# Retention and a mixture of four experts on one core: expert outputs added up in DRAM by accumulating DMAs, and two more down projections in seven products

## The chip, the cores and the metric

The kernel runs on one core of a Trainium2 chip. The metric is the device time of one execution in microseconds. Before the change three runs gave 520.82, 521.08 and 521.61 us; the median is 521.08.

A core has several engines that run side by side and wait for one another through semaphores: PE (TensorE, matrix products into PSUM), PEld (TensorE's load of the stationary operand), DVE (VectorE, elementwise), ACT (ScalarE, elementwise, with a scale per partition), POOL (GpSimd, elementwise on SBUF only) and SP (SyncE, which here only issues DMAs). Each engine executes its own instructions in the order in which the program lists them. DMAs are issued from a queue of SP, ACT or POOL.

## The reference, cut to what matters

```python
# attention, for each of 8 batches and 8 heads: q, k, v are 576 x 64
scores = (q @ k.T) / sqrt(64)
ret = scores * gamma[h] ** (i - j) where i >= j, else 0
x = (ret @ v), heads side by side          # 4608 tokens x 512

# mixture of 4 experts on every token
p = domain_probs / (domain_probs.sum(-1) + 1e-9)
for e in range(4):
    h = maximum(x @ w1[e], 0)              # 512 -> 1024, "up"
    out += p[:, e:e+1] * (h @ w2[e])       # 1024 -> 512, "down"
```

Every token passes through all four experts, and the output of a token is a sum over the experts of a scaled down projection.

## The kernel before, in words

The 4608 tokens are cut into nine tiles `nt` = 0 to 8 of 512 tokens (`NT`), and each tile into four sub-tiles `ns` of 128 (`NSUB`). Tile and expert together make a stage (nt, e). Tile 0 and stage (1, 0) form the head, where the weights are loaded and the first attention is done. From (1, 1) on one loop runs over the stages, each in two halves g = 0 and 1. A half calls `up_fast`, the up projection of this stage, and in its four gaps (`fill(1)` to `fill(4)`) places a quarter each of the *down* projection of the stage before it.

An up projection computes one 2 x 2 block product in seven products of blocks in place of eight, by sums of blocks that are formed beforehand (`weight_sums`, `token_sums`). A down projection comes in two forms. The classical one, `downs`, takes 32 matmuls of 512 columns per tile and expert (line L541), four sub-tiles one after another. The other, class `Down`, takes seven products: 56 matmuls of 256 columns (L623), plus sums of the weights (`down_sums`, once an expert) and of the hidden layer (`hidden_sum`, L593 to L599, each stage), plus copies on ACT and two additions on DVE (L640). One `Down` covers sub-tiles s and s+2 and takes one half of a stage. The dictionary `begin` says from which tile on an expert's down projections take this form. `owed` lists the weight sums that are still to be formed, each with the earliest stage in which it may run (the last classical user of a block that is overwritten must be done) and the stage before which it must have run; `pay` takes the next one when DVE has a free slot, or all that are due when a stage starts.

The order of the work is written out by hand. Within a half, TensorE does product P, R, then fill 1 (products 1 and 5 of the down projection), P again, Q, fill 2 (6 and most of 2), P again, R, fill 3 (the rest of 2, and 7), P again, fill 4 (3 and 4). ACT copies Q from P (L678) and m5 from R (L680), applies the Relus (L686, L695, L700) and makes the copies of `Down` (L629, L633, L636); DVE forms R = P + m5 (L684), on which the following P product waits, and the fourth quarter of the hidden layer (L692), which POOL clips at zero (L693). In between the class `Chain` feeds attention for later tiles into all engines: casts of loaded q, k and v on POOL (L279, L281), transposes by DMA on SP (L297), scores, states and outputs on TensorE (L328 to L379), masks, running sums, and the writing of x for the tile (L242, ACT). When a tile's x is complete, four token sums (L569 to L572) follow on DVE; at the start of an expert-0 stage all that are left run at once.

A down projection ends with the evacuation from PSUM, in which the result is scaled by p. For expert 0 the scaled result is written into `acc`, one buffer of 128 x 512 for each sub-tile: `Down.out` does the first of its two sub-tiles on DVE (L652) and the second on ACT (L650); `downs` uses ACT (L529). For experts 1 to 3 DVE adds the scaled result to `acc` (L654 in `Down.out`, L531 in `downs`). After expert 3 the buffer is stored to `out` by a DMA from SP (L657, L534). Four buffers (`apool`, bufs = NSUB) serve one tile at a time. The helper `after(ins, dep)` makes one instruction wait for another.

Of the kernel before, what the change touches and what calls it, by code (L numbers as in the profile page):

```python
# [9 lines left out]
FP32 = mybir.dt.float32  # L10
# [4 lines left out]
MULT = mybir.AluOpType.mult  # L15
ADD = mybir.AluOpType.add
# [7 lines left out]
def kernel(  # L24
# [10 lines left out]
    nc = tc.nc  # L35
    B, H, S, D = q.shape
    N, E = moe_domain_probs.shape
    _, Dm, F = moe_w1.shape
# [8 lines left out]
    NFC = F // 128  # L47
    NT = 512
    n_nt = N // NT
    NSUB = NT // 128  # L50
# [8 lines left out]
    att1 = ctx.enter_context(tc.tile_pool(name="att1", bufs=1))  # L59
    att2 = ctx.enter_context(tc.tile_pool(name="att2", bufs=2))  # L60
    hpool = ctx.enter_context(tc.tile_pool(name="hpool", bufs=2))
    apool = ctx.enter_context(tc.tile_pool(name="apool", bufs=NSUB))
    xpool = ctx.enter_context(tc.tile_pool(name="xpool", bufs=3))
    tpool = ctx.enter_context(tc.tile_pool(name="tpool", bufs=1))
    psum = ctx.enter_context(tc.tile_pool(name="psum", bufs=1, space=PSUM))
# [6 lines left out]
    def bank(ring, shape, dtype, name):  # L72
        tag = RINGS[ring][turn[ring] % len(RINGS[ring])]
        turn[ring] += 1
        return psum.tile(shape, dtype, tag=tag, name=name)
# [4 lines left out]
    def after(ins, dep):  # L80
        tc.add_manual_dep(ins.ins, dep.ins.name,
                          mybir.DependencyInfo(mybir.DependencyClass.Sync, mybir.DependencyReason.DATA),
                          reason="start order")
# [58 lines left out]
    w1_sb, w2_sb = [], []  # L142
# [71 lines left out]
    probs = const.tile([128, E, NTT], FP32)  # L214
# [36 lines left out]
    class Att:  # L251


        def __init__(self, b):
            self.b, self.t = b, state[b]
            self.m, self.qkT, self.sT, self.s = {}, {}, {}, {}
# [235 lines left out]
                put_x(nc.vector, slice(2 * u, 2 * u + 2), self.b * S + 256 * hf + c * C, os[c])  # L492


    acc, hTs, tsum, ssum, dsum, hsum = {}, {}, {}, {}, {}, {}

    def up_classical(nt, e, lead=0, cut=NT // 2, pause=False):
# [21 lines left out]
    def downs(nt, e, ring):  # L519

        hT = hTs[nt, e]
        if e == 0:
            acc[nt] = [apool.tile([128, Dm], FP32, tag="acc", name="acc") for _ in range(NSUB)]

        def evacuate(po, ns, cols):
            t = nt * NSUB + ns
            pe, a = probs[:, e, t:t + 1], acc[nt][ns][:, cols]
            if e == 0:
                nc.scalar.activation(a, po, Copy, scale=pe)  # L529
            else:  # L530
                nc.vector.scalar_tensor_tensor(a, po, pe, a, op0=MULT, op1=ADD)  # L531
            if e == E - 1:
                eng = nc.scalar if cols.start else nc.sync
                eng.dma_start(out=out[t * 128:(t + 1) * 128, cols], in_=a)  # L534

        for ns in range(NSUB):
            w = Dm // 2 if (nt, ns, e) == (n_nt - 1, NSUB - 1, E - 1) else Dm
            for d in range(0, Dm, w):
                po = bank(ring, [128, w], FP32, "po")
                for fc in range(NFC):  # L540
                    nc.tensor.matmul(po, lhsT=hT[:, fc, ns * 128:(ns + 1) * 128],  # L541
                                     rhs=w2_sb[e][:, fc, d:d + w], start=(fc == 0), stop=(fc == NFC - 1))
                    yield None if fc < NFC - 1 else lambda: evacuate(po, ns, slice(d, d + w))

    def down_groups(nt, e):
        for f in downs(nt, e, "mm"):
            if f:
                f()
                yield
# [51 lines left out]
    class Down:  # L601
# [2 lines left out]

        def __init__(self, nt, e, s, tags=("o0", "o1")):
            self.nt, self.e, self.s, self.tags = nt, e, s, tags
            if e == 0 and s == 0:
                acc[nt] = [apool.tile([128, Dm], FP32, tag="acc", name="acc") for _ in range(NSUB)]

        def product(self, i, part=slice(0, NFC // 2)):  # L610
            hT, h, w, t = hTs[self.nt, self.e], hsum[self.nt, self.e], w2_sb[self.e], dsum[self.e]
# [28 lines left out]
            nc.vector.tensor_tensor(o, i, x, op=ADD)  # L640

        def out(self, i, halves=(slice(0, 2),)):
            ns = 2 * i + self.s
            t, po = self.nt * NSUB + ns, (self.V, self.W)[i]
            pe = probs[:, self.e, t:t + 1]
            for x in halves:
                cols = slice(x.start * HD, x.stop * HD)
                a, src = acc[self.nt][ns][:, cols], po[:, x].rearrange("p a d -> p (a d)")
                if self.e == 0 and i == 1:
                    nc.scalar.activation(a, src, Copy, scale=pe)  # L650
                elif self.e == 0:
                    nc.vector.tensor_scalar_mul(a, src, pe)  # L652
                else:
                    nc.vector.scalar_tensor_tensor(a, src, pe, a, op0=MULT, op1=ADD)  # L654
                if self.e == E - 1:
                    eng = nc.scalar if len(halves) == 1 and x.start else nc.sync
                    eng.dma_start(out=out[t * 128:(t + 1) * 128, cols], in_=a)  # L657

    def up_fast(nt, e, g, fill, window, sums):

# [315 lines left out]
    def stage(nt, e):  # L976
        return nt * E + e

    begin = {1: (1, 1), 2: (1, 2), 3: (2, 3), 0: (3, 0)}
    owed = [((1, 1), (2, 0), s0[3])]  # L980
    for e in (3, 0):

# [12 lines left out]
    for nt, e in [(nt, e) for nt in range(1, n_nt) for e in range(E)][1:]:  # L995
        fast = before >= begin[before[1]]
        fill_classical = None if fast else downs(*before, "po")
        while pay(nt, e, late=True):
            pass
# [142 lines left out]
```

## Time and profile before

| | before |
|---|---|
| median of three runs | 521.08 us |
| the profiled execution, in all | 521.82 us |
| its span | 520.1 us |
| TensorE busy | 505.5 us (97%) |
| VectorE busy | 388.8 us (75%) |
| ScalarE busy | 308.7 us (59%) |
| GpSimd busy | 196.1 us (38%) |
| stores of `out` from SP | 32 of 256 KB, median 2.9 us to landing; 8 of 128 KB, 1.8 us |
| DMA traffic | 54.24 MB, mean 104 GB/s |

The profile is of one execution. Its span begins with the first instruction and ends with the last; the execution's own time is 1.7 us longer. Busy time is the time in which an engine has an instruction under way. Matmuls overlap with one another, so that the duration of one (273 ns for 256 columns) is longer than the distance to the next; the pace is read from runs of several. A few matmul records are missing from the trace (214 of 224 in group L541). In a group's row the numbers after the bar are busy us, mean ns of one, and the idle time of the engine ahead of these instructions with what ended it.

### The profile page before, as it was taken

What the parts mean: (1) busy time and instruction counts of PE and PEld (TensorE: products, weight loads), DVE (VectorE), ACT (ScalarE), POOL (GpSimd) and SP (SyncE); (2) the same over time, 40 slices, a digit from 0 to 9 for tenths busy, and PEclk for the clock granted to TensorE, in tenths of its full rate; (3) what the DMA queues carried; (4) which work ended last, traced back from release to release, by engine and by line L of the source; (5) the groups of instructions that cost most, each with busy time, mean ns of one, the idle gap of its engine ahead of it and who ended that gap; (6) DMA issues with size and microseconds to landing.
All of it is one profiled execution on the core that took longest, in us unless ns stands there. A gap on an engine that the chain in (4) does not pass through costs nothing.

```text
span 520.1 us, 12551 instructions
## 1 busy us (share of the span) xinstructions
PE 505.5 (97%) x4871; PEld 401.6 (77%) x4886; DVE 388.8 (75%) x720; ACT 308.7 (59%) x637; POOL 196.1 (38%) x299
## 2 busy tenths in 40 slices
PE   8999999999999999999999999999999999999995
PEld 3644455678667878888888888888888888888884
DVE  6624579877646888779877987887788878787776
ACT  3462264666446756666666666766666667666661
POOL 6702275644433444444443543354345310000010
PEclk9999999999999999999999999999999999999999
DMA  9999998926183145525463538433941020011002
GB/s 239 187 208 201 199 204 184 160 48 113 42 203 62 42 101 134 137 57 114 95 159 72 112 70 196 72 89 65 204 95 42 13 80 2 2 41 42 2 1 82
DMA packets 149836, 54.24 MB, mean 104 GB/s; under 512 B 131308, under 2 KB 144620, under 8 KB 149776
## 3 DMA queue, kind: packets, MB, share of 16 engines
q1 hardware_dynamic: 142448, 45.05, 40.1%
q0 software_dynamic: 7328, 8.39, 9.5%
q8 instruction: 38, 0.62, 0.5%
q14 instruction: 22, 0.18, 0.1%
HBM read 45.16 MB, written 9.44 MB: 105 GB/s over the span
## 4 chain that ended last, share of the span: by engine, by line
PE 89%; DVE 7%; issue 2%; DMA 1%; ACT 0%; DVEq 0%; SPq 0%
PE upP L672 20%; PE downV L623 18%; PE downW L623 13%; PE upR L672 10%; PE po L541 8%; PE ph L500 6%; PE upQ L672 5%; PE s L328 2%; DVE acc L654 1%; PE oc L379 1%; PE kvp L346 1%; DVE upR L684 1%; PE oc L376 1%; DMA raw<-in_q_dram 1%; DVE sT L333 1%
## 5 line engine op out<-in xcount | busy, mean ns | idle before, releaser
L672 PEld LDWEIGHTS <-wt 128*128 128x128 bf16 x992 | 94.9, 98 | 18.0 <-issue 3.8
L623 PEld LDWEIGHTS <-hT 128*128 128x128 bf16 x928 | 90.8, 98 | 11.1 <-issue 0.6
L693 POOL TENSOR_SCALAR hT<-hT 128x512 bf16<-128x512 bf16 x62 | 38.3, 618 | 160.5 <-DVE hT L692 160.4
L672 PEld LDWEIGHTS <-wsum 128*128 128x128 bf16 x744 | 72.7, 98 | 12.2 <-issue 2.6
L623 PE MATMUL downV<-wt,hT 128*128 128x256 bf16 x464 | 78.4, 273 | 0.4 <-DVE acc L654 0.4
L672 PE MATMUL upP<-xT,wt 128*128 128x256 bf16 x496 | 74.4, 272 | 2.1 <-DVE upR L684 1.7
L623 PEld LDWEIGHTS <-hsum 128*128 128x128 bf16 x696 | 67.8, 98 | 8.7 <-DVE hsum L593 0.3
L684 DVE TENSOR_TENSOR upR<-upP,m 128x512 f32<-128x512 f32 x62 | 43.1, 696 | 35.8 <-PE upP L672 22.1
L700 ACT ACTIVATE hT<-upP 128x512 bf16<-128x512 f32 x62 | 37.0, 597 | 53.0 <-PE upP L672 39.2
L695 ACT ACTIVATE hT<-upR 128x512 bf16<-128x512 f32 x62 | 37.0, 597 | 32.7 <-PE upR L672 32.6
L541 PE MATMUL po<-wt,hT 128*128 128x512 bf16 x214 | 52.1, 379 | 0.6
L678 ACT ACTIVATE upQ<-upP 128x512 f32<-128x512 f32 x62 | 36.3, 586 | 26.0 <-PE upP L672 25.9
L340 POOL TENSOR_SCALAR_AFFINE_SELECT sT<-sT 128x512 bf16<-128x512 bf16 x24 | 15.2, 634 | 96.1 <-ACT sT L339 80.4
L654 DVE SCALAR_TENSOR_TENSOR acc<-downV,probs,acc 128x512 f32<-128x512 f32 (+1 forms) x48 | 34.6, 726 | 22.5 <-PE downV L623 22.4
L686 ACT ACTIVATE hT<-upQ 128x512 bf16<-128x512 f32 x62 | 37.0, 597 | 22.3 <-PE upQ L672 22.3
L692 DVE TENSOR_TENSOR hT<-upP,m 128x512 bf16<-128x512 f32 x62 | 42.8, 690 | 6.5 <-PE upP L672 4.7
L516 ACT ACTIVATE hT<-ph 128x512 bf16<-128x512 f32 x40 | 23.5, 597 | 29.1 <-PE ph L500 28.2
L672 PE MATMUL upR<-tsum,wsum 128*128 128x256 bf16 x248 | 37.2, 272 | 2.3 <-DVE tsum L569 2.3
L680 ACT ACTIVATE m<-upR 128x512 f32<-128x512 f32 x62 | 36.8, 594 | 2.2 <-PE upR L672 2.2
L672 PE MATMUL upP<-tsum,wt 128*128 128x256 bf16 x248 | 37.3, 273 | 0.1
L672 PE MATMUL upP<-tsum,wsum 128*128 128x256 bf16 x248 | 37.2, 273 | 0.0
L672 PE MATMUL upR<-xT,wsum 128*128 128x256 bf16 x248 | 37.2, 273 | 0.0
(136 smaller groups left out, 974.2 us busy)
## 6 DMA issues: line engine op xcount, KB each, us to landing
out_dram<-acc SPq DMA_DIRECT2D x32, 256.0 KB, 2.9
wt<-in_moe_w_dram POOLq DMA_DIRECT2D x6, 1024.0 KB, 26.2
raw_k<-in_k_dram SPq DMA_DIRECT2D x24, 256.0 KB, 3.3
raw_q<-in_q_dram SPq DMA_DIRECT2D x24, 256.0 KB, 3.6
raw_v<-in_v_dram SPq DMA_DIRECT2D x24, 256.0 KB, 3.8
raw<-in_k_dram SPq DMA_DIRECT2D x8, 256.0 KB, 5.6
raw<-in_q_dram SPq DMA_DIRECT2D x8, 256.0 KB, 5.8
raw<-in_v_dram SPq DMA_DIRECT2D x8, 256.0 KB, 5.5
```

The costliest lines, as they stand in the source:

```text
L541: nc.tensor.matmul(po, lhsT=hT[:, fc, ns * 128:(ns + 1) * 128], rhs=w2_sb[e][:, fc, d:d + w], start=(fc == 0), stop=(fc == NFC - 1))
L623: nc.tensor.matmul(o, lhsT=l[:, k, self.s * 128:(self.s + 1) * 128], rhs=r[:, k], start=(i == 1 and k == 0), stop=(k == NFC // 2 - 1), ski ...
L654: nc.vector.scalar_tensor_tensor(a, src, pe, a, op0=MULT, op1=ADD)
L672: nc.tensor.matmul(ps[:, l], lhsT=wa(kc)[:, f:f + 128], rhs=xa(kc), start=(start and l == 0 and kc == 0), stop=(kc == 1), skip_group_check ...
L678: nc.scalar.activation(Q, P, Copy)
L680: nc.scalar.activation(m5, R_, Copy)
L684: nc.vector.tensor_tensor(R_, P, m5, op=ADD)
L686: nc.scalar.activation(hT[:, lo, t0], Q, Relu)
L692: nc.vector.tensor_tensor(h22, P, m5, op=ADD)
L693: nc.gpsimd.tensor_scalar(h22, h22, float("inf"), 0.0, op0=MIN, op1=MAX)
L695: nc.scalar.activation(hT[:, lo, t1], R_, Relu)
L700: nc.scalar.activation(hT[:, hi, t0], P, Relu)
```

## The change

For tiles 1 to 7 the experts are no longer added up in SBUF. Each expert's scaled output is written into a fresh buffer that holds a pair of sub-tiles, 128 x 2 x 512, of which there are two (`apool`, bufs = 2, the same bytes as before). When both sub-tiles of a pair are written, `send` issues a DMA of 512 KB: for expert 0 a plain store from SP, for experts 1 to 3 an accumulating DMA from GpSimd's queue, which adds to what lies in `out`. An accumulating DMA waits until the DMAs of the expert before it on the same rows have landed. A pair is (s, s+2) in the seven-product form, and (0, 1) or (2, 3) in the classical form.

With nothing to add, the evacuation of experts 1 to 3 in these tiles takes the form of expert 0: the first sub-tile of a pair on DVE, the second on ACT, and in `downs` all on ACT. The stores after expert 3 fall away there. Tiles 0 and 8 (`on_chip`) keep their sums in SBUF and their stores of 128 rows. In `downs` the splitting of the very last evacuation into two halves goes; the last tile doesn't use `downs`.

Last, `begin` moves by one tile for two experts, so that the down projections of (1, 3) and (2, 0) take seven products in place of the classical form. The stages that `pay` goes by follow from `begin`: the weight sums of experts 3 and 0 fall due four stages earlier, and their last one may run four stages earlier.

```diff
-    apool = ctx.enter_context(tc.tile_pool(name="apool", bufs=NSUB))
+    apool = ctx.enter_context(tc.tile_pool(name="apool", bufs=2))
...
+    out_rows = out.rearrange("(x p) d -> p x d", p=128)
+    sent = {}
+
+    def on_chip(nt):
+        return nt in (0, n_nt - 1)
+
+    def out_pair(nt, e, pair, j):
+        if e == 0 or not on_chip(nt):
+            acc[nt, j] = apool.tile([128, 2, Dm], FP32, tag="acc", name="acc")
+        return acc[nt, j]
+
+    def send(nt, e, pair, j):
+        x = slice(nt * NSUB + pair[0], nt * NSUB + pair[1] + 1, pair[1] - pair[0])
+        if e == 0:
+            i = nc.sync.dma_start(out=out_rows[:, x, :], in_=acc[nt, j])
+        else:
+            i = nc.gpsimd.dma_start(out=out_rows[:, x, :], in_=acc[nt, j], accum_op=ADD)
+            for p, d in sent[nt, e - 1]:
+                if set(p) & set(pair):
+                    after(i, d)
+        sent.setdefault((nt, e), []).append((pair, i))
...
     def downs(nt, e, ring):
...
-            if e == 0:
+            if e == 0 or not on_chip(nt):
                 nc.scalar.activation(a, po, Copy, scale=pe)
             else:
                 nc.vector.scalar_tensor_tensor(a, po, pe, a, op0=MULT, op1=ADD)
-            if e == E - 1:
-                eng = nc.scalar if cols.start else nc.sync
-                eng.dma_start(out=out[t * 128:(t + 1) * 128, cols], in_=a)
+            if not on_chip(nt):
+                if ns % 2:
+                    send(nt, e, pair, j)
+            elif e == E - 1:
+                nc.sync.dma_start(out=out[t * 128:(t + 1) * 128, :], in_=a)
...
         def out(self, i, halves=(slice(0, 2),)):
...
-                if self.e == 0 and i == 1:
+                if e and on_chip(nt):
+                    nc.vector.scalar_tensor_tensor(a, src, pe, a, op0=MULT, op1=ADD)
+                elif i == 1:
                     nc.scalar.activation(a, src, Copy, scale=pe)
-                elif self.e == 0:
+                else:
                     nc.vector.tensor_scalar_mul(a, src, pe)
-                else:
-                    nc.vector.scalar_tensor_tensor(a, src, pe, a, op0=MULT, op1=ADD)
-                if self.e == E - 1:
+                if e == E - 1 and on_chip(nt):
                     eng = nc.scalar if len(halves) == 1 and x.start else nc.sync
                     eng.dma_start(out=out[t * 128:(t + 1) * 128, cols], in_=a)
+            if i == 1 and not on_chip(nt):
+                send(nt, e, pair, j)
...
-    begin = {1: (1, 1), 2: (1, 2), 3: (2, 3), 0: (3, 0)}
+    begin = {1: (1, 1), 2: (1, 2), 3: (1, 3), 0: (2, 0)}
```

More of the change, by code (lines that the diff above doesn't have):

```diff
@@ L521, in downs, with evacuate @@
         hT = hTs[nt, e]
-        if e == 0:
[L523 to L528, printed above, removed]
+        def evacuate(po, ns):
+            t, pair, j = nt * NSUB + ns, (ns // 2 * 2, ns // 2 * 2 + 1), ns // 2
+            a = (acc[nt, j] if ns % 2 else out_pair(nt, e, pair, j))[:, ns % 2]
+            pe = probs[:, e, t:t + 1]
+            if e == 0 or not on_chip(nt):
                 nc.scalar.activation(a, po, Copy, scale=pe)
@@ L531, in evacuate @@
                 nc.vector.scalar_tensor_tensor(a, po, pe, a, op0=MULT, op1=ADD)
-            if e == E - 1:
-                eng = nc.scalar if cols.start else nc.sync
-                eng.dma_start(out=out[t * 128:(t + 1) * 128, cols], in_=a)
-        for ns in range(NSUB):
[L537 to L543, printed above, removed]
+            if not on_chip(nt):
[3 more added lines that the diff above has]
+                nc.sync.dma_start(out=out[t * 128:(t + 1) * 128, :], in_=a)
+        for ns in range(NSUB):
+            po = bank(ring, [128, Dm], FP32, "po")
+            for fc in range(NFC):
+                nc.tensor.matmul(po, lhsT=hT[:, fc, ns * 128:(ns + 1) * 128],
+                                 rhs=w2_sb[e][:, fc, :], start=(fc == 0), stop=(fc == NFC - 1))
+                yield None if fc < NFC - 1 else lambda: evacuate(po, ns)
     def down_groups(nt, e):
@@ L606, in __init__ @@
             self.nt, self.e, self.s, self.tags = nt, e, s, tags
-            if e == 0 and s == 0:
-                acc[nt] = [apool.tile([128, Dm], FP32, tag="acc", name="acc") for _ in range(NSUB)]
         def product(self, i, part=slice(0, NFC // 2)):
@@ L642, in out @@
         def out(self, i, halves=(slice(0, 2),)):
-            ns = 2 * i + self.s
-            t, po = self.nt * NSUB + ns, (self.V, self.W)[i]
-            pe = probs[:, self.e, t:t + 1]
+            nt, e, j, pair = self.nt, self.e, self.s, (self.s, self.s + 2)
+            if i == 0:
+                out_pair(nt, e, pair, j)
+            t, po, acc_ = nt * NSUB + pair[i], (self.V, self.W)[i], acc[nt, j][:, i]
+            pe = probs[:, e, t:t + 1]
             for x in halves:
                 cols = slice(x.start * HD, x.stop * HD)
-                a, src = acc[self.nt][ns][:, cols], po[:, x].rearrange("p a d -> p (a d)")
-                if self.e == 0 and i == 1:
+                a, src = acc_[:, cols], po[:, x].rearrange("p a d -> p (a d)")
+                if e and on_chip(nt):
+                    nc.vector.scalar_tensor_tensor(a, src, pe, a, op0=MULT, op1=ADD)
+                elif i == 1:
                     nc.scalar.activation(a, src, Copy, scale=pe)
-                elif self.e == 0:
+                else:
                     nc.vector.tensor_scalar_mul(a, src, pe)
-                else:
-                    nc.vector.scalar_tensor_tensor(a, src, pe, a, op0=MULT, op1=ADD)
-                if self.e == E - 1:
+                if e == E - 1 and on_chip(nt):
                     eng = nc.scalar if len(halves) == 1 and x.start else nc.sync
                     eng.dma_start(out=out[t * 128:(t + 1) * 128, cols], in_=a)
+            if i == 1 and not on_chip(nt):
+                send(nt, e, pair, j)
     def up_fast(nt, e, g, fill, window, sums):
```

## The prediction

> **What bounds the kernel now.** I read the page's first part, then the chain of work that ended last, then groups by shape, the table of windows, and the timeline around each break in TensorE's row.
>
> ```profile
> span 520.1 us, 12551 instructions
> ...
> PE 505.5 (97%) x4871; PEld 401.6 (77%) x4886; DVE 388.8 (75%) x720; ACT 308.7 (59%) x637; POOL 196.1 (38%) x299
> ...
> PE 89%; DVE 7%; issue 2%; DMA 1%; ACT 0%; DVEq 0%; SPq 0%
> ```
>
> TensorE sets the end: 97% busy, 89% of the chain. A busy PE row can hide waste, so I compare matmul spacing in the chain (start us, length us, engine, what):
>
> ```profile
> 151.00 0.86 PE po L541 x4
> ...
> 163.76 0.87 PE downV L623 x8
> ...
> 190.29 0.53 issue
> 191.23 0.66 DVE acc L654
> 192.28 0.60 PE upR L672 x4
> ...
> 246.52 0.66 DVE acc L654
> 248.09 0.48 issue
> 248.57 0.70 DVE upR L684
> 249.31 0.60 PE upP L672 x4
> ```
>
> Four matmuls of 512 columns take 0.86 us, eight of 256 columns 0.87: one pace, 0.42 ns a column. From stage (7,2) on halves repeat every 6.11 us, 56 x 0.109. So TensorE can only be helped by fewer columns or by removing the breaks where DVE, the second engine of the chain, makes it wait. The other two pieces show such breaks: both pass through an `acc` evacuation on DVE.
>
> **What the Trainium skill says.** (1) "DMA: Bandwidth & Descriptors", Rules for kernel authors: accumulating DMAs go through GpSimd, and whoever touches the same bytes must wait for the earlier DMA's semaphore. That is the added wait; the trace of before has no accumulate. (2) "Collectives: The Full Stack", The bandwidth ceiling: the add in a DMA costs because it "needs **two source reads**", halving the rate (ratio 1.93). No run here shows it yet. (3) Same DMA page, Anatomy of one DMA: about 2.0 us + bytes/436e3 for a DMA from GpSimd; the trace's plain stores of 256 KB land in 2.9 us (SP's queue), the formula gives 2.6. (4) "SBUF — State Buffer", Who interferes with whom: two-port DVE modes lock GpSimd out of writing descriptors, and a DVE op with two SBUF inputs contends with GpSimd reads. The trace agrees on the second: the hidden sum L593 takes 0.41 to 1.25 us. The scaling that replaces L654 reads PSUM and keeps its 751 ns, so I see no lock.
>
> **The change part by part.** Rows used, by shape:
>
> ```profile
> L693 POOL TENSOR_SCALAR hT<-hT 128x512 bf16<-128x512 bf16 x62 | 38.3, 618 | 160.5 <-DVE hT L692 160.4
> ...
> L654 DVE SCALAR_TENSOR_TENSOR acc<-downW,probs,acc 128x512 f32<-128x512 f32 x44 | 32.7, 742 | 0.0
> ...
> L652 DVE TENSOR_SCALAR acc<-downV,probs 128x512 f32<-128x512 f32 x12 | 9.0, 751 | 7.4 <-PE downV L623 7.2
> ...
> L650 ACT ACTIVATE acc<-downW,probs 128x512 f32<-128x512 f32 x12 | 8.3, 689 | 2.2 <-PE downW L623 2.2
> ...
> L153 POOL DMA_DIRECT2D wt<-in_moe_w_dram x4 | 3.6, 907 | 0.0
> ```
>
> *Two down projections in seven products.* Classical: 32 matmuls of 512 columns, 8 x 0.865 = 6.92 us. Seven products: 56 of 256, 7 x 0.87 = 6.11. Two of them: **-1.62 us**, on the bound engine. Price: per projection DVE adds hidden sums (four of 0.43 and two of 0.69) and four adds of 0.43, ACT six copies of 0.38. Stages (2,0) and (2,1) have room: in 137 to 154 us DVE idles 0.5 to 1.7 us before most operations. The last weight sums of experts 3 and 0 (L572, 0.68 each, at 149.1 and 171.4 before) must come earlier. DVE slots are there: one at 103.3 now takes expert 0's first sum, two at 114.1 and 115.0, and at 128 to 129.5 DVE idles 1.60 us, where expert 0's last two (0.98 + 0.68) fit. Without that cover they run in one piece at the start of (2,1), up to 1.7 us on TensorE.
>
> *Evacuations.* In tiles 1 to 7, experts 1 to 3, the first of each pair changes L654 (751 ns) for a scaling (751): nothing. The second leaves DVE (spacing 0.66 us) for ACT (0.69, spacing 0.57), 42 times. What it frees is read from the timeline, as start of the late matmul minus the start its predecessor's pace allows:
> - The expert-0 stages start with product R waiting for the first token sum, behind two evacuations: 1.12 us lost at 135.64, 1.46 at 192.28. At 192.28 the second evacuation (0.66) goes: -0.66. At 135.64 it goes too, but (1,3) being fast now puts a hidden sum (0.43) there: -0.22. Sum **-0.88**.
> - DVE late with L684, so that the third P product waits: 0.33 (116.68), 0.21 (207.66), 0.25 (249.31), 0.56 (262.10), 0.25 (303.74), 0.21 (316.18), 0.21 (370.04). All but one are preceded by gapless DVE work and are shorter than 0.66, so they vanish. At 262.10 DVE idles 0.46 us before L599 for a reason I can't read; I take half, between 0 and 0.56. Sum 0.33+0.21+0.25+0.28+0.25+0.21+0.21 = **-1.74**. The breaks at 130.23, 379.24 and 382.23 (0.2 each) have other releasers; the last two and the one at 494 I leave.
>
> Does ACT stall instead? Behind the added operation stand Q's copy L678 and the copies m5 and L629; the next P product waits for L678. Expert 0's pairs already do this, even with an attention copy in front:
>
> ```profile
> 266.25 0.69 ACT L650 ACTIVATE acc<-downW,probs 128x512 f32<-128x512 f32 x1
> 266.82 0.61 ACT L678 ACTIVATE upQ<-upP 128x512 f32<-128x512 f32 x1
> ...
> 267.70 0.60 PE L672 MATMUL upP<-tsum,wsum 128*128 128x256 bf16 x4
> ```
>
> L678 ends at 267.43, 0.27 us ahead of 267.70, and TensorE keeps its pace. Cost 0, with 0.27 us of cover.
>
> *Transfers.* POOL issues 42 accumulates (two pairs, three experts, seven tiles). Unknown issue time: at least the 0.77 to 0.91 us of weight loads, at most twice that; I take 0.9, 38 us in all on an engine 38% busy. Behind a waiting issue stand the casts, the state copies L369 and the Relu L693. The issue waits for ACT's evacuation, done about 1 us into the next half, and ends near 2 us; L693 is wanted at about 4 us, and it idles 160.5 us waiting for DVE. Where three casts (2.7 us) come first the issue ends near 3.5. Cover 0.5 us or more: cost 0. SP: 28 stores of 256 KB become 14 of 512 KB at expert 0, after an ACT wait; its loads and transposes queue behind as they did behind the expert-3 stores, and transposes are issued some 7 us before use and land in 3.3. Cost 0, up to a few tenths a tile if they slip.
>
> Landing of an accumulate, an estimate from the pages above: 2.0 + 2 x 524288/436e3 = 4.4 us; at one read 3.2, at four times the plain time 6.8. The buffer comes round after two halves, 12.2 us, of which 2 (issue early) to 3.5 go to evacuation and issue: 8.7 us or more are left. The next expert's accumulate asks its predecessor's landing even later. Cost 0.
>
> ```profile
> 364.00:377.00 13.00, 12.95 (x137) 11.21 (x136) 9.85 (x19) 8.03 (x18) 5.08 (x8) 1.00 1.05 205
> ...
> 468.00:481.00 13.00, 13.00 (x122) 11.65 (x120) 9.66 (x20) 8.57 (x19) 1.23 (x2) 1.00 0.11 42
> ```
>
> The columns before the last are the granted clock and the share of the DMA engines. The second window holds one tile's 512 KB of stores: 0.11 x 13 = 1.4 us of sixteen engines. With two reads 2.9 us per half of 6.1 to 7.2: +0.4 to +0.47 on a mean of 0.45 from 104 to 429 us; the head runs at 1.2. It fits on average; at 364 to 377 it queues for a while.
>
> **The sum** against the profiled execution: span 520.1 - 1.62 - 0.88 - 1.74 = 515.9; with the 1.7 us around it (521.82 in all) 517.6. The median of the runs, 521.08, is 0.74 below that execution: 521.08 - 4.24 = **516.8 us**.
>
> **Rivals.**
> - *Only the products count.* The freed DVE time is lost to another wait: POOL's issues push L693 back in the 21 of 62 halves where POOL was busy before it; 0.9 us late against 0.66 saved leaves TensorE where it was. For: DVE reads L693's result directly. Against: the idle 160 us. 521.08 - 1.62 = 519.5; chance 0.12.
> - *Contention gives all back.* Accumulates delay transposes and loads in the busy bursts, six batches at about 0.7 us: near 521; chance 0.05.
> - *Accumulates don't land in time: slower.* The place is the first evacuation of each pair on DVE, waiting for its buffer, with POOL blocked on the predecessor. It decides from a landing of 8.7 us on where casts come first, 10 us elsewhere. Each us beyond lengthens a stage by 1 us, some 24 stages: at 11 us landing 24 us, giving 541; already 0.2 us over eats the gain. For: no accumulate is in this trace, and one read-modify-write per 2 KB row could cost more than two reads. Against: twice the estimate is needed. Chance 0.11.
>
> **How the numbers follow.** My forecast 0.72 (its own range 515.0 to 518.6: all breaks gone and three small ones too, or half of the DVE ones left). The first rival reaches 519.5, the second 521. The range 514.8 to 521.2 leaves out the slow rival and a little beyond. What a measurement of this kernel can tell from no change is 0.2%, 1.0 us. Faster 0.84, within 0.2% 0.05, slower 0.11.
>
> **What would show it.** Right: L541 matmuls fall by 64, L623 grow by 112; L654 falls by some 80, and an ACT row of 40 to 50 evacuations appears; upR's wait at expert 0 of tile 3 is below 0.9 us; no DVE wait for a DMA on `acc`; POOL issues near 0.9 us; L693's idle is still over 100 us. Wrong: DVE or POOL waiting for out_dram DMAs, issues of 2 us or more, new TensorE breaks behind L678 or at the attention scores (L328), a landing above 8 us.

## The result, and the profile after

The changed kernel's median is 517.01 us (516.56 to 518.52, 4 runs) against 521.29 us (520.82 to 521.61, 4 runs) for the kernel before, measured beside it: a ratio of 0.9924, with a 95% interval of 0.9900 to 0.9947. It is faster by 4.1 to 4.3 us; the prediction was 516.8 us.

The profiled execution of the changed kernel took 516.57 us, its span is 514.8 us. From the page's first part, the share of each queue's DMAs (queue, packets, MB, share of 16 engines), and the chain by engine:

```profile
span 514.8 us, 12812 instructions
...
PE 501.4 (97%) x4934; PEld 405.5 (79%) x4934; DVE 376.1 (73%) x700; ACT 334.5 (65%) x689; POOL 247.0 (48%) x341
...
q1 hardware_dynamic: 142224, 45.05, 47.0%
q0 software_dynamic: 18752, 30.41, 37.2%
...
PE 92%; DVE 4%; DMA 1%; issue 1%; POOL 0%; SPq 0%; DVEq 0%; POOLq 0%
```

TensorE still sets the end; DVE's share of the chain fell from 7% to 4%. GpSimd's busy time grew by 51 us, and its DMA queue's share from 9.5% to 37.2%. Groups by shape, beside those shown of before (busy us, mean ns of one, then the idle time ahead and what ended it):

```profile
L514 POOL DMA_DIRECT2D out_dram<-acc x42 | 51.3, 1221 | 30.9 <-ACT acc L675 24.1 <-ACT upQ L703 4.7 <-DVE xT L595 1.9
...
L677 DVE TENSOR_SCALAR acc<-downV,probs 128x512 f32<-128x512 f32 x56 | 41.9, 748 | 30.1 <-PE downV L644 29.8
L675 ACT ACTIVATE acc<-downW,probs 128x512 f32<-128x512 f32 x56 | 38.6, 689 | 9.2 <-PE downW L644 9.2
L718 POOL TENSOR_SCALAR hT<-hT 128x512 bf16<-128x512 bf16 x62 | 38.0, 613 | 110.7 <-DVE hT L717 110.6
```

Lines have moved by some twenty: L677 and L675 are the scalings by DVE and ACT (12 each before, 56 now), L718 is the Relu on GpSimd, L514 the accumulating DMA, L709 forms R, L592 to L595 the weight and token sums, L616 to L622 the hidden sums. The landing times (KB each, median us from issue to landing) are in the last part of the page:

```profile
out_dram<-acc POOLq DMA_DIRECT2D x42, 512.0 KB, 6.7
out_dram<-acc SPq DMA_DIRECT2D x14, 512.0 KB, 3.5
```

No engine waits for these DMAs in the list of waits. The chain of work around the starts of stages (2,0) and (3,0), which answer to 135.64 and 192.28 before:

```profile
131.81 1.05 POOL km L279
132.86 0.61 DVE hsum L616
133.47 0.55 DVE tsum L592
134.01 0.04 issue
134.06 0.60 PE upR L697 x4
...
187.60 0.41 DVE hsum L616
188.02 0.35 DVE tsum L592
188.37 0.04 issue
188.41 0.60 PE upR L697 x4
```

The second is as predicted: one evacuation less, 0.80 us lost in place of 1.46. The first is not: the two sums take 0.61 us each, and the loss is 1.20 us where 0.90 was predicted.

**Where the time went.** The head's length differs from execution to execution (stage (1,1) starts between 89.7 and 91.6 us in the kernels below, though only the one with other casts changes the head), so I compare three pieces: from the start of stage (1,2) to the start of the last half (what the change works on; I call this the loop), the tail from there to the span's end, and the medians. As the start of a half I take the start of the fourth and last matmul of its first P product. Loop and tail are of one profiled execution of each kernel. The last column is the ratio to the kernel before, run beside each.

| kernel | from (1,2), us | tail, us | median, us | ratio, 95% |
|---|---|---|---|---|
| before | 394.64 | 18.30 | 521.29 | |
| changed | 390.21 | 18.92 | 517.01 | 0.9924 (0.9900 to 0.9947) |
| changed, run again | 391.77 | 18.97 | 518.79 | 0.9938 (0.9915 to 0.9960) |
| products only | 392.69 | 18.31 | 518.73 | 0.9946 (0.9926 to 0.9965) |
| accumulating only | 391.22 | 18.97 | 519.23 | 0.9961 (0.9948 to 0.9974) |
| second evacuation on DVE | 393.62 | 19.26 | 520.58 | 0.9987 (0.9977 to 0.9997) |
| token sum first | 390.61 | 18.94 | 517.89 | 0.9927 (0.9905 to 0.9948) |
| plain stores from GpSimd | 390.23 | 19.01 | 517.40 | 0.9920 (0.9893 to 0.9948) |
| plain stores from SP | 389.66 | 18.59 | 516.20 | 0.9905 (0.9888 to 0.9922) |
| casts with one input | 389.52 | 18.98 | 516.32 | 0.9902 (0.9882 to 0.9922) |
| sums spread, stores on two queues | 389.52 | 18.47 | 516.94 | 0.9903 (0.9869 to 0.9938) |

From (1,2) on the changed kernel is 4.43 us shorter, for a predicted 4.24; the tail gives 0.62 back. A second run of the changed kernel, on another chip, gained less: 2.87 us in the loop of its profiled execution, and 2.5 us in the medians. What differed is told below, under the changed kernel again. In all these kernels the engines' last operation ends 14.9 us after the start of the last half, so the growth of the tail comes later: 0.26 us of it until the last store has landed, 0.37 us after that.

### The profile page after: what moved, and what is told of

It is laid out like the page before. It is cut to its first block, busy times and chain, and to the rows that moved or that the text cites. A ratio compares the mean times of both kernels' runs of the same rounds, so it can differ in the third digit from the quotient of the medians.

```text
span 514.8 us, 12812 instructions
## 1 busy us (share of the span) xinstructions
PE 501.4 (97%) x4934; PEld 405.5 (79%) x4934; DVE 376.1 (73%) x700; ACT 334.5 (65%) x689; POOL 247.0 (48%) x341
## 3 DMA queue, kind: packets, MB, share of 16 engines
q0 software_dynamic: 18752, 30.41, 37.2%
## 4 chain that ended last, share of the span: by engine, by line
PE 92%; DVE 4%; DMA 1%; issue 1%; POOL 0%; SPq 0%; DVEq 0%; POOLq 0%
PE upP L697 21%; PE downV L644 20%; PE downW L644 15%; PE upR L697 10%; PE ph L525 7%; PE po L564 7%; PE upQ L697 5%; PE s L328 2%; PE oc L379 1%; PE oc L376 1%; PE kvp L346 1%; DMA raw<-in_q_dram 1%; DVE sT L469 1%; DVE acc L673 1%; DVE upR L709 0%
## 5 line engine op out<-in xcount | busy, mean ns | idle before, releaser
L644 PEld LDWEIGHTS <-hT 128*128 128x128 bf16 x992 | 97.1, 98 | 11.8 <-issue 0.6
L718 POOL TENSOR_SCALAR hT<-hT 128x512 bf16<-128x512 bf16 x62 | 38.0, 613 | 110.7 <-DVE hT L717 110.6
L644 PE MATMUL downV<-wt,hT 128*128 128x256 bf16 x496 | 83.9, 273 | 0.4 <-DVE acc L673 0.4
L644 PEld LDWEIGHTS <-hsum 128*128 128x128 bf16 x744 | 72.4, 98 | 9.3 <-DVE hsum L616 0.3
L709 DVE TENSOR_TENSOR upR<-upP,m 128x512 f32<-128x512 f32 x62 | 43.3, 698 | 46.5 <-ACT downW L650 41.2
L514 POOL DMA_DIRECT2D out_dram<-acc x42 | 51.3, 1221 | 30.9 <-ACT acc L675 24.1
L677 DVE TENSOR_SCALAR acc<-downV,probs 128x512 f32<-128x512 f32 x56 | 41.9, 748 | 30.1 <-PE downV L644 29.8
L675 ACT ACTIVATE acc<-downW,probs 128x512 f32<-128x512 f32 x56 | 38.6, 689 | 9.2 <-PE downW L644 9.2
L697 PE MATMUL upR<-tsum,wsum 128*128 128x256 bf16 x248 | 37.2, 273 | 1.7 <-DVE tsum L592 1.7
L703 ACT ACTIVATE upQ<-upP 128x512 f32<-128x512 f32 x62 | 37.0, 597 | 2.5 <-PE upP L697 2.3
L644 PE MATMUL downV<-dsum,hsum 128*128 128x256 bf16 x248 | 37.2, 273 | 0.0
```

The costliest lines, as they stand in the source:

```text
L514: i = nc.gpsimd.dma_start(out=out_rows[:, x, :], in_=acc[nt, j], accum_op=ADD)
L644: nc.tensor.matmul(o, lhsT=l[:, k, self.s * 128:(self.s + 1) * 128], rhs=r[:, k], start=(i == 1 and k == 0), stop=(k == NFC // 2 - 1), ski ...
L697: nc.tensor.matmul(ps[:, l], lhsT=wa(kc)[:, f:f + 128], rhs=xa(kc), start=(start and l == 0 and kc == 0), stop=(kc == 1), skip_group_check ...
L703: nc.scalar.activation(Q, P, Copy)
L709: nc.vector.tensor_tensor(R_, P, m5, op=ADD)
L718: nc.gpsimd.tensor_scalar(h22, h22, float("inf"), 0.0, op0=MIN, op1=MAX)
```

## The experiments

**Each part alone.** Products only is the kernel before with the new `begin`; accumulating only is the changed kernel with the old one.

```diff
-    begin = {1: (1, 1), 2: (1, 2), 3: (2, 3), 0: (3, 0)}
+    begin = {1: (1, 1), 2: (1, 2), 3: (1, 3), 0: (2, 0)}
```

> The kernel before with the second part alone: down projections (1,3) and (2,0) in seven products, experts still added up in SBUF. My theory (the parts add up): -1.62 us from the matmuls, +0.43 us because a hidden sum now stands ahead of the first token sum at the start of (2,0) with both evacuations still on VectorE: about -1.2 us, ratio 0.9977; the break ahead of product R there grows from 1.1 to about 1.5 us. Rival (the products need the relief): VectorE can't hold the hidden sums in these stages, breaks of 1 us and more appear in (2,0) and (2,1), ratio 1.000 or above.

> The changed kernel with the first part alone: accumulating DMAs for tiles 1 to 7, but the down projections (1,3) and (2,0) classical as before. My theory: the DVE breaks go (-0.66 at each of the two token-sum waits, -1.4 to -1.7 at L684's), nothing else changes: about -2.8 us, ratio 0.9946. Rival (the accumulates cost something that the products hide): less than -1 us, ratio above 0.998.

The products alone shorten the loop by 1.95 us, more than their 1.62 of matmuls and than the 1.2 that I expected. The break at R in (2,0) grows from 1.12 to 1.46 us as expected, and a new one of 0.21 appears at 150, but other breaks shrink: that at 262.10 falls from 0.56 to 0.21, and those at 379, 382 and 494 (0.17, 0.16, 0.21) are gone. Why these went wasn't tried; the ones at 379 and 382 come and go in the kernels below, and are there in the changed kernel. Accumulating alone shortens the loop by 3.42 us (2.8 expected) and lengthens the tail by 0.67.

The parts add up to 5.37 where both together give 4.43. With accumulation in place, stage (2,0) takes 13.50 us with the classical projection and 13.43 with the seven products: the break at R there is 0.49 us with the one and 1.20 with the other, so that most of one product gain is lost. Without accumulation it grew by 0.34, so this is 0.37 of the 0.94 that are missing. Another 0.56 lie in breaks that each part takes away by itself (0.35 at 262.10, 0.21 at 494). The rest is a balance of small breaks that differ from execution to execution.

**The second evacuation back on DVE.** Accumulation stays, and experts 1 to 3 give ACT nothing.

```diff
-                elif i == 1:
+                elif i == 1 and e == 0:
                     nc.scalar.activation(a, src, Copy, scale=pe)
```

> The changed kernel, but for experts 1 to 3 of tiles 1 to 7 both evacuations of a pair stay on VectorE (scalings, 0.75 us each); the accumulating DMAs and the products stay. My theory (the gain of the first part is VectorE's freed time): the breaks of before come back, as with the products alone: about -1.2 us against before, ratio 0.9977, and ScalarE's evacuations fall from 56 to 14. Rival (the gain comes from the output leaving SBUF, or from the smaller number of stores on SyncE's queue): as fast as the changed kernel, ratio 0.992.

Of the 4.43 us, 1.02 are left, and the breaks of before are back: 1.46 us at R in (2,0) and (3,0), 0.2 to 0.3 at R in later stages. That is 0.93 less than the products give alone: accumulation that doesn't relieve DVE costs time (0.56 of it is a break ahead of the attention scores; the medians, 520.58 against 518.73, say the same). DVE's timeline in (2,0) (start us, length us, engine and instruction) shows what stands ahead of the first token sum:

```profile
133.32 0.75 DVE L677 TENSOR_SCALAR acc<-downV,probs 128x512 f32<-128x512 f32 x1 [1.00 <-PE downV L644]
133.99 0.42 DVE L616 TENSOR_TENSOR hsum<-hT 128x512 bf16<-128x512 bf16 x1
134.32 0.74 DVE L677 TENSOR_SCALAR acc<-downW,probs 128x512 f32<-128x512 f32 x1
134.99 0.42 DVE L592 TENSOR_TENSOR tsum<-xT 128x512 bf16<-128x512 bf16 x1
```

So the gain of accumulation is DVE's time, not anything in the DMAs themselves. Note the 0.42 us of the two sums here; in the changed kernel the token sum begins 0.45 us sooner in the stage, the hidden sum at the same place, and both take 0.61.

**The token sum first.** If the break at R is only the order of work on DVE, the first token sum could go ahead of the evacuation.

```diff
@@ the last half of a tile
+        if (e, g) == (E - 1, 1):
+            chain.put_late()
@@ its fill(4), ahead of the evacuation
+                if (e, g) == (E - 1, 1):
+                    n = len(front)
+                    tokens(nt + 1)
+                    if len(front) > n:
+                        front.pop(0)()
```

> The changed kernel with an earlier first token sum: in the second half of each expert-3 stage, x is written ahead of the last Relu, and the first token sum of the next tile stands ahead of the evacuation on VectorE, where it idles about 1 us. If the two breaks left at the start of (2,0) and (3,0) (1.20 and 0.80 us) are due to the place of this sum in VectorE's order, both go: 2.0 us below the changed kernel, ratio to before about 0.9885. Rival (something else is late next, x itself or the hidden sums for products 5 and 6): less than 1 us below it, ratio 0.991.

No gain that can be measured. R in (2,0) is 0.55 us late in two breaks in place of 1.20, but 0.69 us come back at the third P product. GpSimd's and DVE's rows of the timeline there:

```profile
133.01 1.04 POOL L279 TENSOR_TENSOR km<-raw_k,gk 128x512 bf16<-128x512 f32 x1
...
133.13 1.21 DVE L592 TENSOR_TENSOR tsum<-xT 128x512 bf16<-128x512 bf16 x1 [0.76 <-ACT xT L242]
```

The moved sum takes 1.21 us, not 0.42. It ran beside a cast on GpSimd that multiplies k by a factor. In (3,0) the 0.80 us at R are gone, and 0.66 come back at the third P product.

**Casts with one input.** The same sight explains the break of 0.33 us at 116.68, which I had predicted to go and which stayed in every kernel above. DVE and GpSimd at the corresponding places, first in the kernel before, then in the changed kernel:

```profile
113.41 1.04 POOL L279 TENSOR_TENSOR qm<-raw_q,gq 128x512 bf16<-128x512 f32 x1
...
114.11 0.89 DVE L570 TENSOR_TENSOR dsum<-wt,dsum 128x1024 bf16<-128x1024 bf16 x1
```

```profile
111.94 1.04 POOL L279 TENSOR_TENSOR qm<-raw_q,gq 128x512 bf16<-128x512 f32 x1
...
111.97 1.55 DVE L592 TENSOR_TENSOR dsum<-wt 128x1024 bf16<-128x1024 bf16 x1
```

With the second evacuation gone the weight sum starts 0.66 us sooner in its stage, then takes 1.55 us where the weight sum at the corresponding place before (another one, of the same size) took 0.89: what was freed is used up. To test it I leave the factor out of GpSimd's casts in L279, so that they become copies (q and k are not scaled by gamma in this kernel).

```diff
-            if n in gain:
+            if n in gain and eng is not nc.gpsimd:
                 eng.tensor_tensor(o, i, gain[n][:, c, :]...to_broadcast([128, H, D]), op=MULT)
             else:
                 eng.tensor_copy(o, i)
```

> Left out: the factor gk or gq by which GpSimd multiplies k and q while it casts them (L279); the cast itself stays, with one input in place of two, at nearly the same duration (1.04 us against 1.07 for the cast of v). Theory: at the break of 0.33 us that stayed at 115 us, the DVE time freed by the second evacuation (0.66) was eaten by the weight sum behind it, which took 1.55 us in place of 0.89 because it ran beside two of GpSimd's casts with two inputs. Then this sum takes 0.9 to 1.0 us here, R is formed some 0.6 us sooner and the break goes. At 134 us the hidden sum and the token sum ran beside L369, which has one input already; they keep about 0.6 us each and the break stays within 1.0 to 1.2 us. In all the loop is 0.3 to 0.6 us shorter than in the changed kernel, ratio near 0.991. Rival: the second input is not what slows DVE, the sum keeps 1.5 us and the break 0.33 us, ratio as that of the changed kernel (0.992 to 0.994).

The same two engines in this kernel, there and at the start of (2,0):

```profile
111.82 0.61 POOL L281 CAST qm<-raw_q 128x512 bf16<-128x512 f32 x1
...
112.33 0.68 DVE L592 TENSOR_TENSOR dsum<-wt 128x1024 bf16<-128x1024 bf16 x1
112.38 1.10 POOL L281 CAST vm<-raw_v 128x512 bf16<-128x512 f32 x1
...
132.37 0.85 POOL L369 CAST sbd<-ksum 64x256 bf16<-64x256 f32 x2
...
132.87 0.63 DVE L616 TENSOR_TENSOR hsum<-hT 128x512 bf16<-128x512 bf16 x1
133.43 0.41 DVE L592 TENSOR_TENSOR tsum<-xT 128x512 bf16<-128x512 bf16 x1
```

The weight sum takes 0.68 us, and the break is gone; stage (1,2) takes 13.36 in place of 13.69 us. At (2,0), where the hidden sum runs beside L369 in both kernels, it keeps about the same time, 0.63 us; the token sum behind it, which starts when L369 is over, takes 0.41, and the break is 1.02. From (1,2) on the loop is 0.69 us shorter than the changed kernel's. One thing I had wrong: I had put the cast with one input at the duration of the cast of v; it takes 0.61 us in place of 1.04. So the test shows that the casts are what stretches the sum, but doesn't by itself tell their second input from their length. The sum now begins 0.05 us ahead of the cast of v and takes no longer for it, while the next weight sum, which begins within that cast, takes 0.98.

The traces settle it. Take all weight, token and hidden sums (two operands in SBUF) that start after 90 us in the eleven profiled executions, the one with everything added twice left out. In 375 of them a GpSimd instruction was under way at the start and had 0.2 us or more to go. Each of these sums took longer than its undisturbed time (0.42 or 0.68 us) by what was left of that instruction less 0.14 us, to within 0.01 us. This holds for the 220 beside a GpSimd instruction with two inputs and for the 155 beside one with one input (casts, the Relu, the mask) alike. The 22 sums that met only GpSimd instructions that began after them kept their time. So the second input matters only as it makes the cast longer; what counts is which of the two starts first, and how much of it is left. At 116.68 the freed time let the sum begin 0.03 us after the cast of q instead of 0.70 us after it.

**The addition, and the queue.** One kernel keeps the 42 DMAs on GpSimd's queue but without the addition, a second issues them from SP. In both only the last expert's output remains in `out` for tiles 1 to 7.

```diff
-            i = nc.gpsimd.dma_start(out=out_rows[:, x, :], in_=acc[nt, j], accum_op=ADD)
+            i = nc.gpsimd.dma_start(out=out_rows[:, x, :], in_=acc[nt, j])   # first kernel
+            i = nc.sync.dma_start(out=out_rows[:, x, :], in_=acc[nt, j])     # second kernel
```

> The changed kernel with plain stores in place of the accumulating DMAs, still from GpSimd's queue with the same waits; the last expert's output alone stays in tiles 1 to 7, nothing is added. It prices the addition: landing should fall from 6.7 us (5.7 undisturbed) by about 1.5 us, one reading of 512 KB, and the issue from 1.22 to about 0.9 us. My theory (both are hidden): time as the changed kernel, ratio to before 0.990 to 0.9945. Rival (the accumulates' load on the DMA engines gives part of the gain back through late transposes): 1 us or more below the changed kernel, ratio below 0.9905, and no break of TensorE ahead of the scores.

> Left out: the addition, as in the kernel with plain stores from GpSimd's queue; the stores of experts 1 to 3 go from SP's queue instead, so that the output holds the last expert alone. Theory: GpSimd's issues are hidden (cost 0 in the prediction), so the loop is as long as with plain stores from GpSimd, 406.2 us from the first to the last half, within 0.4, if SP's transposes behind the waiting stores don't slip. The idle time of L718 grows from 110 us to about 150. Rival one: GpSimd's issues do cost, and the loop is 0.5 to 1.5 us shorter. Rival two: a store that waits for its evacuation holds up the transposes and loads behind it on SP's queue, new breaks ahead of the scores (L328) appear, and the loop is 0.5 to 2 us longer.

First kernel, group and landing:

```profile
L514 POOL DMA_DIRECT2D out_dram<-acc x42 | 32.6, 777 | 30.8 <-ACT acc L675 26.3
...
out_dram<-acc POOLq DMA_DIRECT2D x42, 512.0 KB, 3.9
```

The addition costs 0.44 us of GpSimd per issue (1221 against 777 ns) and 2.8 us of landing (6.7 against 3.9), and yet the loop is as long as in the better of the changed kernel's two profiled executions, 390.23 against 390.21 us. Against the other one, on the same chip as this kernel, it is 1.54 us shorter, and the median is 1.4 us lower (517.40 against 518.79): there the rival's "1 us or more" is met, though not its ratio. The next experiment shows where that time lies. Issuing from SP saves another 0.57: three breaks, at 311, 374 and 377 us (0.19, 0.17, 0.16), are not there. Whether GpSimd's issues cause them isn't shown: the last two were in the kernel before as well, when GpSimd issued no stores, and none of the three is in the kernel with accumulation alone, where GpSimd issues all 42. GpSimd's issues cost 0 to 0.6 us. SP's transposes didn't slip behind the waiting stores. The tail falls by 0.42 to 18.59 us: more than half of the tail's growth goes with the use of GpSimd's queue in the loop. Of the rest, and of why, nothing was tried.

**The changed kernel again.** It was run a second time, on the chip on which the plain stores from GpSimd and the last two experiments below ran.

> The changed kernel once more, beside the others of this call, as what they are compared with: 0.992 of before. If the place of the work decides alone, its loop from stage (1,2) to the last half takes 390.2 us again, within 0.5; if the DMA engines' load shows, breaks of TensorE ahead of the scores come and go and the loop is longer by their sum.

The profiled execution has the breaks of the first and three more, ahead of the attention scores: 0.36 us at 206, 0.25 at 260, 1.23 at 315. The chain there:

```profile
306.47 8.08 DMA qkT<-km
314.55 0.05 issue
314.59 0.40 PE s L328 x8
```

A transpose took 8.08 us from issue, and TensorE waited for it. Medians of the transposes of q and k (24 each, in the list of DMA issues) are 6.4 and 4.4 us here, 5.9 and 4.3 in the first execution, 3.7 and 2.9 before, 4.0 and 3.2 with plain stores from GpSimd. From (1,2) on the profiled executions of the two kernels with plain stores have no break of 0.1 us or more ahead of the scores. In the seven with accumulating DMAs, the one with everything added twice left out, such breaks sum to 0 (casts with one input), 0.11 (the first execution), 0.38, 0.47, 0.56, 0.85 and 1.84 us. The kernel before and products only have none. So the additions delay transposes, by an amount that differs from execution to execution, and what that costs TensorE differs with it.

**Each output added twice.** To load the path of the slow rival, each accumulating DMA is issued a second time, and the second waits for the first (experts 1 to 3 count double in `out`).

```diff
+        if e:
+            again = nc.gpsimd.dma_start(out=out_rows[:, x, :], in_=acc[nt, j], accum_op=ADD)
+            after(again, i)
+            i = again
```

> The changed kernel, but every accumulating DMA is issued twice, the second waiting for the first, so that experts 1 to 3 of tiles 1 to 7 are added twice and the output is another one. A buffer is then free some 13 us after its first issue in place of 6.7. My theory (landing is hidden by 2.9 us or more, and not by 6.7): VectorE's first evacuation waits for a DMA, about 2 us a stage over some 24 stages, and GpSimd is blocked about 5 us in every half: 550 us or more. Rival (landing has no deadline that matters): within 5 us of the changed kernel.

703.38 us in one run. The longest waits (engine, what waited, for what: us, times, longest):

```profile
POOL out_dram L519 <- DMA out_dram<-acc: 191.4, 32, 7.9
DVE hsum L620 <- POOL hT L722: 108.1, 27, 8.9
...
PE downV L648 <- DVE hsum L620: 84.5, 14, 9.9
```

GpSimd stands 191 us at the second DMA, its Relu (L722 here) comes late, the hidden sum that reads it comes late, and TensorE waits for that. DVE waited for a buffer 7 times, 6.0 us in all, and ACT twice, 1.7 us. So nearly all the waiting is on GpSimd, and not at the buffer where I expected it. But the experiment puts it there: the second DMA stands right behind the first and waits for it. In the changed kernel an accumulating DMA waits for one issued a stage earlier, which had landed at least 4.8 us before in both profiled executions, while the nearest write to a buffer came 2.8 us after the landing. By these figures a later landing would hold up DVE there first, as the rival said. At which landing time it would, this experiment doesn't give.

**A version that is likely faster than both.** The token sum first, as above; then the third of the token sums, which nobody needs yet, moved behind the second gap; and every second of the last stores issued from ACT's queue.

```diff
-                    eng = nc.scalar if len(halves) == 1 and x.start else nc.sync
+                    eng = nc.scalar if x.start else nc.sync
@@ fill 2
+            if i == 2 and third:
+                third.pop()()
@@ start of an expert-0 stage
+        if e == 0 and len(front) == 3:
+            front.pop(0)()
+            front.pop(1)()
+            third.append(front.pop(0))
```

> The earlier token sum (as in e4), and besides: the third token sum of (2,0) and (3,0) moved behind R = P + m5, so that TensorE's third P product waits less, and of the last stores every second one issued from ScalarE's queue, which is idle then, in place of SyncE's alone. Theory (the length of VectorE's list ahead of R = P + m5 is what is late, and SyncE's 0.49 us per store sets the end): the breaks at the start of (2,0) and (3,0) fall from 2.0 us to 0.5 to 1.0 in sum, the tail by 0.5 to 0.9: 1.5 to 2 us below the changed kernel, ratio to before about 0.989. Rival (the same time moves to the next product, and the landing of the stores sets the end): less than 0.7 us below it.

516.94 us against 518.79 for the changed kernel on the same chip. The break at (3,0) is gone (stage (3,0) takes 12.23 us, TensorE's pace without a break), 0.9 us in four pieces are left at (2,0), and the tail is 0.50 shorter. The two intervals overlap (0.9869 to 0.9938, 0.9915 to 0.9960), so the medians' difference of 1.85 us is likely but not certain, and part of it lies in the breaks ahead of the scores (0.38 us here, 1.84 there), which this version doesn't address. Against the changed kernel's better execution, on another chip, the loop is 0.69 us and the tail 0.45 us shorter, while the medians are level (516.94 and 517.01).

## Why the prediction was right, step by step

The sum was right: 4.24 us predicted, 4.43 measured from (1,2) on, 4.1 to 4.3 in the medians. The mechanism was right too: with the second evacuation back on DVE most of the gain goes. That the sum came so close is in part luck. Several of its terms were off, and balanced, and the first profiled execution met nearly none of the breaks ahead of the scores; the second run gained 2.5 us in the medians.

- *Products, -1.62.* Right on the bound engine: 64 classical matmuls fewer, 112 of 256 columns more. (7 x 0.87 is 6.09, not 6.11; the 6.11 is the measured length of a half, which has as many matmuls. It makes 0.04 us.) Alone they gave 1.95 with the breaks that went along.
- *Token-sum breaks, -0.88.* At (3,0) exact (1.46 to 0.80). At (2,0) the step failed: 1.12 became 1.20, not 0.90. I took the sums at 0.42 us, their duration where they stood; in the changed kernel each of the two begins while a cast of L369 is under way on GpSimd, and takes 0.61. The prediction had quoted the Trainium skill's "SBUF — State Buffer", Who interferes with whom, on exactly this (a DVE operation with two inputs in SBUF contends with GpSimd's reads) and had applied it to L654's replacement alone, not to the sums behind it. The traces agree with the page and give the size: the rest of the GpSimd instruction less 0.14 us.
- *R breaks, -1.74.* Measured -1.5: those at 207.66, 249.31, 262.10, 303.74 and 370.04 are gone, 262.10 in full where I took half. That at 116.68 stayed at 0.33 for the reason shown by the casts; that at 316.18 shrank from 0.21 to 0.17, and is gone where SP issues the stores. The breaks at 130 and 494 (0.2 each), which I had left, went too. (I gave the one at 130 another releaser; the profile names R = P + m5, L684, for it as well, though DVE had idled 1.6 us ahead of it.) With the products these come to 1.62 + 0.58 + 1.52 + 0.41 = 4.13; the last 0.3 lie in breaks below 0.15 us, which I didn't follow.
- *ACT, 0.* Right: L703, the copy of Q, keeps its place, and no new break behind it appears.
- *GpSimd's issue, 0.9 us, cost 0.* Mis-sized: 1.22 us, within the stated bounds. It cost 0 to 0.6. The Relu idles 110.7 us, over the 100 that was asked for.
- *Landing, 4.4 us.* Mis-sized: median 6.7, close to the upper bound of 6.8, and longest 9.1, past the 8 us that I had named as a sign of failure; nothing waited for it all the same. The price from two reads gave 2.9 us of sixteen engines for one accumulate. The window that held 512 KB of plain stores at a DMA share of 0.11 before holds one accumulate after, at 0.29 (last three columns: clock, DMA share, GB/s):

```profile
468.00:481.00 13.00, 13.00 (x122) 11.65 (x120) 9.27 (x18) 9.60 (x20) 1.21 (x2) 1.00 0.29 42
```

  That is 0.29 x 13 = 3.8 us against 1.4: a factor of 2.6, where the Trainium skill's "Collectives: The Full Stack", The bandwidth ceiling, gives 1.93 for an addition in another setting. The verdict held since the deadline was far: worked out from the starts of L677, every accumulate landed at least 2.9 us before the next write to its buffer.
- *Transfers on SP, 0, up to a few tenths a tile.* This is the term with the least sure size: 0.1 us in the first profiled execution, 1.8 in the second. The contention rival, given a chance of 0.05, is real, but in the executions seen at less than half its price.
- *Tail.* Not costed in the prediction: +0.6 us.
- *The slow rival.* It didn't come about, with 2.8 us or more to spare, and its mechanism was not tested. What adding twice shows is another price: DMAs that make GpSimd wait right behind their predecessor's issue cost some 185 us, far more than 1 us a stage, since the Relu stands behind them.

## What to carry to other kernels

Work that is moved or uncovered takes the duration that it has beside its new neighbours: before a freed slot is counted as a gain, look at whether the next DVE operation reads two operands from SBUF, and whether a GpSimd instruction will be under way when it starts. An accumulating DMA in place of an addition on a busy engine paid here through the engine's time alone, and cost time where that engine got no relief; price it at 1.2 us of GpSimd per issue and over twice the DMA time of a plain store, and make it wait only for DMAs that have long landed, since all of GpSimd's work queues behind it. Give a close sum a second run before calling it exact. Parts that relieve the same wait don't add up.

## What the runs showed of the hardware

- An accumulating DMA of 512 KB from SBUF to DRAM (float32): issue 1.22 us on GpSimd against 0.78 for a plain store, landing 6.7 us (from 5.7 to 9.1) against 3.9 (from 3.2), both medians from GpSimd's queue; plain from SP's queue 3.7.
- DVE sums of two SBUF operands that start while a GpSimd instruction is under way: longer by the rest of that instruction less 0.14 us, whether it has one input or two (375 sums in eleven executions). Two of them: 1.21 us in place of 0.42 (128x512), 1.55 in place of 0.68 (128x1024). Sums that start first keep their time. A DVE operation with one of its two operands in PSUM, the masking of the scores (L333), kept its 0.68 us in all of 129 such cases.
- On GpSimd the cast of a 128x512 tile took 1.04 us with a factor and 0.61 without. The cast of v, of the same shape and without a factor, took 1.10 us in the same kernel where it began 0.05 us after a DVE sum.
- DMA transposes of q and k beside the accumulating DMAs took 5.9 and 4.3 us to landing (medians; 6.4 and 4.4 in a second execution, one of them 8.1), against 4.0 and 3.2 beside plain stores of the same size.
- Kernels whose loop issues stores from GpSimd have a tail of 18.9 to 19.3 us (18.5 where the last stores go out on two queues), and of 18.6 where SP issues them. The kernels before and products only, whose loop stores half as large from SP, have 18.3.
